# Fused causal attention and SwiGLU FFN on one core: normalised x transposed by DMA instead of on TensorE, with its stages spread over the FFN groups

## The chip, the cores and the metric

The kernel runs on one core of a Trainium2 chip. The metric is the device time of one execution in microseconds (us). Most executions of one kernel agree within a fraction of a per cent; medians are quoted.

Engines are named as in the profile: PE is TensorE (matmul), PEld its weight loads, DVE is VectorE, ACT is ScalarE, POOL is GpSimd, SP is SyncE, which here only issues DMAs. "L359" is a line of the kernel that the view belongs to; the same statement has another number in another version. A lower-case q (SPq, POOLq) is the sequencer or DMA queue of that engine. A DMA lands when its data have arrived. "Half clock" is a stretch in which the granted PE clock is 0.5.

## The reference

Eight batches of causal attention, eight heads each, 576 positions, head dimension 64. A decay bias is added to the scores. The outputs of all heads of a position form one row of 512 numbers; the 4608 rows go through an RMS norm and a SwiGLU FFN (512 to 1536 to 512).

```python
def _attn_ref(q, k, v, s):
    scores = scale * np.matmul(q, k.transpose(0, 1, 3, 2))
    s_pos = np.maximum(s, 0.0)
    cum = np.cumsum(s_pos, axis=-1)
    bias = -(cum[:, :, :, None] - cum[:, :, None, :])
    scores = np.where(causal, -1000000000.0, scores + np.minimum(bias, 0.0))
    ...                                     # softmax over keys, then attn @ v

def _moe_ref(x, w_gate, w_val, w_out, rms_g):
    rms = np.sqrt(np.mean(x * x, axis=-1, keepdims=True) + 1e-06)
    xn = x / rms * rms_g
    g = xn @ w_gate
    silu = g * (1.0 / (1.0 + np.exp(-g)))
    val = xn @ w_val
    return (silu * val @ w_out).astype(np.float32)
```

## The kernel before

The kernel is a chain of nine stages. Stage c (0 to 8) is one FFN chunk of 512 rows. It has two parts. In the first, FFN1, PE computes gate and value products in 12 groups of 16 matmuls (a group covers 256 hidden units for 256 rows in the "halves" plan, so groups 0 to 5 need the chunk's first 256 rows and groups 6 to 11 the last 256; in the "whole" plan a group covers all 512 rows). In the second, 48 output matmuls are interleaved with the attention of batch c+1: scores, exp, mask, attention times V. A batch has 576 rows and a chunk 512, so chunk c can start when the first rows of batch c are normalised; the rest are normalised while FFN1 already runs.

The way of a block of 128 rows from attention to FFN1: x_blk holds the attention output with rows on the partitions. ACT squares and sums it, POOL takes the power -1/2, DVE scales it, and then it must be turned so that the model dimension lies on the partitions (xnT), because FFN1 contracts over that dimension. Before the change PE turns it, by four transposing matmuls into PSUM, and DVE copies it out with rms_g multiplied in:

```python
def att_square(a, tb):
    nc.scalar.activation(out=sq_scr[:, 0:DM], in_=a.x[:, tb, :], func=AF.Square,
                         accum_out=a.ss[:, tb : tb + 1])

def att_alpha(a, t0, t1):
    ...                                              # POOL: mean + eps, then
    nc.gpsimd.tensor_tensor(out=y, in0=m, in1=mhalf[:, 0 : t1 - t0], op=ALU.pow)

def att_scale(a, tb):
    nc.vector.tensor_scalar(out=a.x[:, tb, :], in0=a.x[:, tb, :],
                            scalar1=a.al[:, 1, tb : tb + 1], scalar2=None, op0=ALU.mult)

def att_out(a, tb):
    p0 = 64 if tb == 4 else 0
    X = ps_x()                                       # PSUM
    for cc in range(CC):
        nc.tensor.matmul(X[:, cc, :], lhsT=a.x[:, tb, cc * 128 : (cc + 1) * 128],
                         rhs=ident_bf, is_transpose=True,
                         start=(cc == 0), stop=(cc == CC - 1))
    c0 = a.b * S + tb * 128
    nc.vector.tensor_tensor(
        out=xnT[:, :, c0 : c0 + 128 - p0], in0=X[:, :, p0:128],
        in1=g_sb.unsqueeze(2).to_broadcast([128, CC, 128 - p0]), op=ALU.mult)

def ffn1_group(Ht, t0, o, n, f0):
    ...
    nc.tensor.matmul(P[:, j, i * n : (i + 1) * n],
                     lhsT=w[:, cc, fb * 128 : (fb + 1) * 128],
                     rhs=xnT[:, cc, t0 + o : t0 + o + n], ...)
```

Everything that is not PE work of the FFN is a "filler": a pair of a position (0 to 1 through FFN1) and a function, emitted after the FFN1 group at that position. In a stage c, POOL issues the loads of k and q of batch c+2, SP the loads of v, POOL scales v of batch c+1 by the decay (`prep_v`), and SP issues two large DMA transposes that turn K and Q of batch c+1 (`dma_transpose`):

```python
elif c + 1 < B:
    fillers += prep_fillers(c + 1, 0.4, 0.98)       # prep_v on POOL at 0.2 to 0.8
    ...
    for w in range(2):
        dma_transpose(c + 1, w)                      # K and Q, at the stage's start
if c + 2 < B:
    for w in range(2):
        fillers.append((0.1, lambda b=c + 2, w=w: load_kq(b, w)))   # five issues each, POOL
    fillers.append((0.1, lambda b=c + 2: load_v(b, nc.sync)))       # five issues, SP
...
Ht = ffn1(c, halves if c < 4 else whole, fillers)
```

## Time and profile before

| | before |
|---|---|
| time, median of three runs | 396.05 us (395.88 to 397.04) |
| span of the profiled run | 394.0 us |
| PE busy | 355.1 us, 90% |
| mean granted PE clock | 0.989 |
| first FFN1 matmul (end of the load phase) | 29.0 us |
| stage 0 / stages 1 to 5 / stage 6 | 55.2 / 39.5 to 39.7 each / 41.4 us |

The page's first part gives busy time and share of the span for each engine. Its second part cuts the span into 40 slices; a digit is the busy share in tenths, and in the row PEclk it is the clock granted to PE, in tenths of full speed.

```profile
PE 355.1 (90%) x2870; PEld 210.5 (53%) x2907; DVE 219.9 (56%) x438; ACT 203.6 (52%) x327; POOL 172.0 (44%) x267
...
PE   2779993999999999999999999999979999999993
...
PEclk9999999799999999999999999999999999999998
```

PE is the bottleneck: from the fourth slice on it is over 90% busy everywhere, except in the last slice, in the 30th (a wait of 2.0 us for H_sb in stage 6) and in the seventh, which is very poor. The waits view of PE, where a line says how long PE sat idle in front of an instruction and which instruction ended it, says what that slice is:

```profile
PE psAV L322 <- POOL E L300: 7.2, 2, 7.0
...
PE psX L351 <- DVE x_blk L327: 4.6, 7, 0.7
PE psD L366 <- DVE H_sb L373: 2.0, 1, 2.0
```

One wait of 7.0 us lies in stage 0, where POOL masks E only after it has scaled v, and v had landed late. The granted clock falls after it (the 7 in the PEclk row). Otherwise a stage's waits are short: the transposes into psX wait some 0.66 us for the last attention output.

The timeline of PE in stage 3 shows what the transposes cost. The columns are start, duration, engine, line, operation, output and inputs, count.

```profile
167.01 0.39 PE L351 MATMUL psX<-ident_bf,x_blk 128*128 128x128 bf16 x4
167.42 1.03 PE L366 MATMUL psD<-xnT,wg_sb 128*128 128x256 bf16 x8
...
169.17 0.39 PE L351 MATMUL psX<-ident_bf,x_blk 128*128 128x128 bf16 x4
169.39 1.04 PE L366 MATMUL psD<-xnT,wg_sb 128*128 128x256 bf16 x8
...
201.69 0.40 PE L351 MATMUL psX<-ident_bf,x_blk 128*128 128x128 bf16 x4 [0.66 <-DVE x_blk L327]
```

Eight matmuls of 256 columns take 0.87 us from start to start; four transposes push the next group back by 0.22 us (169.17 to 169.39), or 0.41 in the first of these lines (167.01 to 167.42). There are five blocks in a batch and eight batches. A saving of 9 us of issue, with the gaps round the last two blocks of each stage, is what the change can hope for on PE.

### The profile page before, as it was taken

The page shows a single profiled execution, that of the slowest core. Times are in us where ns is not written, and L with a number is a line of the kernel's source. Part 1 is how long each engine was busy: PE and PEld are TensorE (multiplying, and loading weights), DVE is VectorE, ACT ScalarE, POOL GpSimd, SP SyncE. Part 2 cuts the span into 40 slices and gives each one's busy share as a digit, 9 for nine tenths or more (in the row PEclk, how much of TensorE's full clock was granted, in tenths as well). Part 3 has the DMA queues.
Part 4 walks back from the last instruction along what each step waited for, and adds up shares of the span by engine and source line. Part 5 has one row for each costly group of instructions (what it writes and reads, how often), then busy time and mean ns, then how long its engine had stood idle before and what let it go on. Part 6 is the DMA issues. An engine that isn't in the chain of part 4 may idle for free.

```text
span 394.0 us, 7348 instructions
## 1 busy us (share of the span) xinstructions
PE 355.1 (90%) x2870; PEld 210.5 (53%) x2907; DVE 219.9 (56%) x438; ACT 203.6 (52%) x327; POOL 172.0 (44%) x267
## 2 busy tenths in 40 slices
PE   2779993999999999999999999999979999999993
PEld 1457871469746974698454445444434454444441
DVE  6774960675377546754675467546763585424431
ACT  2664564564486448644864486458635773302310
POOL 8553639459145924592459245924540240000000
PEclk9999999799999999999999999999999999999998
DMA  8999999039923992299529932993260010011011
GB/s 118 212 202 169 196 209 141 28 88 154 176 66 85 147 175 79 66 152 142 126 72 155 171 85 72 152 171 89 69 119 2 27 56 29 0 56 52 0 45 71
DMA packets 128905, 41.60 MB, mean 106 GB/s; under 512 B 116960, under 2 KB 123616, under 8 KB 128864
## 3 DMA queue, kind: packets, MB, share of 16 engines
q0 software_dynamic: 63840, 16.52, 48.1%
q1 hardware_dynamic: 65024, 24.53, 31.5%
q8 instruction: 25, 0.41, 0.4%
q14 instruction: 16, 0.13, 0.1%
HBM read 37.90 MB, written 9.44 MB: 120 GB/s over the span
## 4 chain that ended last, share of the span: by engine, by line
PE 71%; POOL 8%; DMA 7%; ACT 6%; DVE 5%; issue 2%; POOLq 0%; ACTq 0%
PE psD L366 41%; PE psO L394 18%; DMA v_nat<-in_v_dram 7%; PE psAV L322 6%; PE psD L293 4%; ACT E L298 2%; ACT L298 2%; ACT sq_scr L334 2%; DVE x_blk L344 2%; PE psX L351 2%; POOL v_nat L118 1%; POOL E L300 1%; POOL vw L258 1%; DVE x_blk L327 1%; POOL xnT L111 1%
## 5 line engine op out<-in xcount | busy, mean ns | idle before, releaser
L373 DVE TENSOR_TENSOR H_sb<-S_sb,psD 128x512 bf16<-128x512 bf16 x108 | 74.1, 687 | 93.6 <-ACT S_sb L372 93.3
L372 ACT ACTIVATE S_sb<-psD 128x512 bf16<-128x512 f32 x108 | 64.4, 597 | 114.8 <-PE psD L366 105.5
L366 PE MATMUL psD<-xnT,wg_sb 128*128 128x256 bf16 (+1 forms) x615 | 111.5, 315 | 2.9 <-DVE H_sb L373 2.0
L366 PE MATMUL psD<-xnT,wv_sb 128*128 128x256 bf16 (+1 forms) x623 | 112.0, 315 | 0.3
L394 PE MATMUL psO<-wout_sb,H_sb 128*128 128x512 bf16 x405 | 103.0, 382 | 1.4
L300 POOL TENSOR_SCALAR_AFFINE_SELECT E<-E 128x512 bf16<-128x512 bf16 x64 | 40.6, 636 | 98.0 <-ACT E L298 95.2
L366 PEld LDWEIGHTS <-wv_sb 128*128 128x128 bf16 x624 | 61.4, 98 | 33.1
L366 PEld LDWEIGHTS <-wg_sb 128*128 128x128 bf16 x624 | 60.4, 99 | 34.0 <-issue 2.5
L298 ACT ACTIVATE E<-psD 128x1024 bf16<-128x1024 f32 x64 | 63.7, 1023 | 17.8 <-PE psD L293 17.5
L394 PEld LDWEIGHTS <-H_sb 128*128 128x128 bf16 x432 | 37.7, 98 | 36.9 <-issue 3.5
L399 DVE COPY osb<-psO 128x512 f32<-128x512 f32 x36 | 24.8, 688 | 30.3 <-PE psO L394 28.6
L322 PE MATMUL psAV<-vw,E 128*128 128x65 bf16 x576 | 32.9, 202 | 9.7 <-POOL E L300 7.2
L322 PEld LDWEIGHTS <-E 128*128 128x128 bf16 x576 | 24.4, 102 | 21.6 <-POOL E L300 14.0
L258 POOL TENSOR_TENSOR vw<-v_nat,wT 128x512 bf16<-128x512 f32 (+1 forms) x35 | 35.4, 1047 | 0.1
L334 ACT ACTIVATE sq_scr<-x_blk 128x512 bf16<-128x512 bf16 x40 | 25.1, 628 | 18.1 <-DVE x_blk L327 17.3
L327 DVE TENSOR_TENSOR x_blk<-psAV,rZ 128x256 bf16<-128x256 f32 (+1 forms) x64 | 31.4, 491 | 2.2
L105 POOL DMA_DIRECT2D k_nat<-in_k_dram x30 | 25.8, 873 | 9.2 <-DMA wout_sb<-in_moe_w_out_dram 6.4
L293 PE MATMUL psD<-QT,KT 64*128 64x256 bf16 (+2 forms) x384 | 27.2, 252 | 1.3 <-ACT E L298 0.9
L293 PEld LDWEIGHTS <-KT 64*128 64x128 bf16 x384 | 13.2, 99 | 27.2 <-issue 25.8
L326 DVE RECIPROCAL rZ<-psAV 128x4 f32<-128x4 f32 (+1 forms) x64 | 11.8, 184 | 28.0 <-PE psAV L322 27.7
L105 POOL DMA_DIRECT2D q_nat<-in_q_dram x30 | 25.4, 870 | 3.6 <-DMA k_nat<-in_k_dram 1.7
L244 DVE TENSOR_REDUCE peak<-QT 128x1 f32<-128x640 bf16 (+1 forms) x32 | 25.3, 792 | 0.0
(77 smaller groups left out, 218.5 us busy)
## 6 DMA issues: line engine op xcount, KB each, us to landing
out_dram<-osb SPq DMA_DIRECT2D x36, 256.0 KB, 2.0
v_nat<-in_v_dram SPq DMA_DIRECT2D x24, 256.0 KB, 10.1
k_nat<-in_k_dram POOLq DMA_DIRECT2D x24, 128.0 KB, 7.6
q_nat<-in_q_dram POOLq DMA_DIRECT2D x24, 128.0 KB, 12.6
v_nat<-in_v_dram POOLq DMA_DIRECT2D x8, 256.0 KB, 12.2
wg_sb<-in_moe_w_gate_dram POOLq DMA_DIRECT2D x2, 768.0 KB, 15.1
wv_sb<-in_moe_w_val_dram POOLq DMA_DIRECT2D x2, 768.0 KB, 18.9
wout_sb<-in_moe_w_out_dram POOLq DMA_DIRECT2D x2, 768.0 KB, 13.1
```

Source lines behind the costliest of these rows:

```text
L105: nc.gpsimd.dma_start(out=dst[0:n, b % 2, sc, :, :], in_=src[b, :, sc * 128 : sc * 128 + n, :].rearrange("h p d -> p h d"))
L258: eng.tensor_tensor(out=vw[0:n, sc, :, 0:64], in0=v_nat[0:n, b % 2, sc, :, :], in1=wb.unsqueeze(2).to_broadcast([n, H, D]), op=ALU.mult)
L293: nc.tensor.matmul(st[:, j, c0 : c0 + q1 - q0], lhsT=keys(a.b, rs, hp, kb), rhs=queries(a.b, rs, hp, q0, q1), start=(i == 0), stop=(i == l ...
L298: nc.scalar.activation(out=E, in_=st, func=AF.Exp, scale=0.125)
L300: nc.gpsimd.affine_select(out=diag, in_=diag, pattern=[[0, 4], [1, 128]], compare_op=ALU.is_ge, fill=0.0, base=0, channel_multiplier=-1)
L322: nc.tensor.matmul(AV[:, j, qb - q0, :], lhsT=E[:, j, c0 : c0 + 128], rhs=vw[:, kb, h, :], start=(j == 0 and i == 0), stop=(j == 1 and i = ...
L327: nc.vector.tensor_tensor(out=a.x[:, q0 : q0 + nq, hp * 128 : (hp + 1) * 128].rearrange("p t (j d) -> p j t d", j=2), in0=AV[:, :, :, 0:64 ...
L334: nc.scalar.activation(out=sq_scr[:, 0:DM], in_=a.x[:, tb, :], func=AF.Square, accum_out=a.ss[:, tb : tb + 1])
L366: nc.tensor.matmul(P[:, j, i * n : (i + 1) * n], lhsT=w[:, cc, fb * 128 : (fb + 1) * 128], rhs=xnT[:, cc, t0 + o : t0 + o + n], start=(i = ...
L372: nc.scalar.activation(out=sl, in_=P[:, 0, :], func=AF.Silu)
L373: nc.vector.tensor_tensor(out=Ht[:, f0 : f0 + m, o : o + n], in0=sl.rearrange("p (i n) -> p i n", i=m), in1=P[:, 1, :].rearrange("p (i n) ...
L394: nc.tensor.matmul(O, lhsT=Ht[:, fb, tb * 128 : (tb + 1) * 128], rhs=wout_sb[:, fb, :], start=(fb == 0), stop=(fb == FB - 1))
```

## The change

The intent is to take the 160 transposes off PE and their evictions off DVE. SP issues a DMA transpose from SBUF to SBUF for each block; rms_g is then applied in the scaling on DVE, as a row broadcast to all partitions. A DMA transpose takes longer to come back, so squares, power and scaling are spread over the early FFN1 groups ("stages"), and loads are moved. The first loads of stage 0 move from position 0.1 to 0.25. The rest of the diff, cut to what matters:

```diff
     def att_scale(a, tb):
-        nc.vector.tensor_scalar(out=a.x[:, tb, :], in0=a.x[:, tb, :],
-                                scalar1=a.al[:, 1, tb : tb + 1], scalar2=None, op0=ALU.mult)
+        nc.vector.scalar_tensor_tensor(out=a.x[:, tb, :], in0=a.x[:, tb, :],
+                                       scalar=a.al[:, 1, tb : tb + 1], in1=g_row,
+                                       op0=ALU.mult, op1=ALU.mult)

     def att_out(a, tb):
         p0 = 64 if tb == 4 else 0
-        X = ps_x()
-        ... four transposing matmuls, eviction on DVE with g_sb ...
+        nc.sync.dma_start_transpose(out=xnT[:, :, c0 : c0 + 128 - p0], in_=a.x[p0:128, tb, :])

+    def table(func):
+        nc.scalar.activation(out=dummy[:, 1:2], in_=dummy[:, 0:1], func=func)
+
+    def attention(b, fl):
+        early = {1: 2, 2: 1, 3: 1}.get(b, 0)
+        a = att_begin(b)
+        table(AF.Exp)                     # the table load, early
+        ... scores now in pairs, AV in pairs, output matmuls between ...
+            if early and u == HP:
+                for tb in range(early):
+                    att_square(a, tb)
+                att_alpha(a, 0, early)
+                for tb in range(early):
+                    att_scale(a, tb)
+                    att_out(a, tb)
+        table(AF.Silu)
+        take(fl, 48)
+        return a
+
+    stages = {0: ((2, 3, 4), ()), 1: ((2, 3, 4), ()), 2: ((1, 2), (3, 4)), 3: ((1, 2), (3, 4))}
+    def tail_fillers(a):                  # default of stages: ((0, 1), (2, 3, 4))
+        f = []
+        g = 0
+        for st in stages.get(a.b, ((0, 1), (2, 3, 4))):
+            if not st:
+                continue
+            for i, tb in enumerate(st):
+                f.append((g + i, lambda tb=tb: att_square(a, tb)))
+            g += len(st) - 1
+            f.append((g, lambda st=st: att_alpha(a, st[0], st[-1] + 1)))
+            for i, tb in enumerate(st):
+                f.append((g + 1, lambda tb=tb: [att_scale(a, tb), att_out(a, tb)]))
+            g += 2
+        return [((p + 0.9) / 12, fn) for p, fn in f]
...
+                if c == 1:
+                    fillers.append((0.3, lambda: load_v(2, nc.sync)))
                 for w in range(2):
-                    dma_transpose(c + 1, w)
+                    fillers.append((0.4, lambda b=c + 1, w=w: dma_transpose(b, w)))
             if c + 2 < B:
                 for w in range(2):
-                    fillers.append((0.1, lambda b=c + 2, w=w: load_kq(b, w)))
-                fillers.append((0.1, lambda b=c + 2: load_v(b, nc.sync)))
+                    fillers.append(((0.24, 0.6)[w], lambda b=c + 2, w=w: load_kq(b, w)))
+                if c:
+                    fillers.append((0.85, lambda b=c + 2: load_v(b, nc.sync)))
...
-            Ht = ffn1(c, halves if c < 4 else whole, fillers)
+            Ht = ffn1(c, halves if c < B else whole, fillers)
```

v of batch 1 is now scaled on DVE, that of later batches on POOL at positions 0.62 to 0.9; `E` gets eight buffers instead of seven.

More of the change, by code (lines that the diff above doesn't have):

```diff
@@ L60 @@
     g_sb = pers.tile([128, CC], fp32, name="g_sb")
+    g_row = pers.tile([128, DM], fp32, name="g_row")
     s_all = pers.tile([BH, S], fp32, name="s_all")
@@ L78 @@
     knrm = pers.tile([128, 1], fp32, name="knrm")
-    mhalf = pers.tile([128, 3], fp32, name="mhalf")
+    mhalf = pers.tile([128, NB], fp32, name="mhalf")
     hones = pers.tile([128, 2], fp32, name="hones")
@@ L83 @@
     ok1 = pers.tile([BH, 2], fp32, name="ok1")
+    dummy = pers.tile([1, 2], fp32, name="dummy")
     flag = pers.tile([1, 1], i32, name="flag")
@@ L93, in ps_av @@
         return pp.tile([128, 2, nq, 65], fp32, name="psAV", tag="AT", bufs=2)
-    def ps_x():
-        return pp.tile([128, CC, 128], bf16, name="psX", tag="AT", bufs=2)
     def ps_t():
@@ L296, in unit_scores @@
                     start=(i == 0), stop=(i == len(groups) - 1))
-        E = a.E[u] = mp.tile([128, 2, DM], bf16, name="E", tag="E", bufs=7)
+        E = a.E[u] = mp.tile([128, 2, DM], bf16, name="E", tag="E", bufs=8)
         nc.scalar.activation(out=E, in_=st, func=AF.Exp, scale=0.125)
@@ L343, in att_scale @@
     def att_scale(a, tb):
-        nc.vector.tensor_scalar(out=a.x[:, tb, :], in0=a.x[:, tb, :],
-                                scalar1=a.al[:, 1, tb : tb + 1], scalar2=None, op0=ALU.mult)
+        nc.vector.scalar_tensor_tensor(out=a.x[:, tb, :], in0=a.x[:, tb, :],
+                                       scalar=a.al[:, 1, tb : tb + 1], in1=g_row,
+                                       op0=ALU.mult, op1=ALU.mult)
     def att_out(a, tb):
         p0 = 64 if tb == 4 else 0
-        X = ps_x()
-        for cc in range(CC):
-            nc.tensor.matmul(X[:, cc, :], lhsT=a.x[:, tb, cc * 128 : (cc + 1) * 128],
-                             rhs=ident_bf, is_transpose=True,
-                             start=(cc == 0), stop=(cc == CC - 1))
         c0 = a.b * S + tb * 128
-        nc.vector.tensor_tensor(
-            out=xnT[:, :, c0 : c0 + 128 - p0], in0=X[:, :, p0:128],
-            in1=g_sb.unsqueeze(2).to_broadcast([128, CC, 128 - p0]), op=ALU.mult)
+        nc.sync.dma_start_transpose(out=xnT[:, :, c0 : c0 + 128 - p0], in_=a.x[p0:128, tb, :])
     def ffn1_group(Ht, t0, o, n, f0):
@@ L415, in prep_fillers @@
         f += spread([lambda i=i: prep_norm(b, i) for i in range(3)], lo, hi)
-        f += spread([lambda sc=sc: prep_v(b, sc, nc.gpsimd) for sc in range(NB)], 0.2, 0.8)
-        f.append((0.8, lambda: prep_w(b, nc.gpsimd)))
-        return f
-    def tail_fillers(a, steps):
-        return [(p, lambda tb=tb: att_out(a, tb)) for p, tb in zip(steps, (2, 3, 4))]
+        f += spread([lambda sc=sc: prep_v(b, sc, nc.vector if b < 2 else nc.gpsimd) for sc in range(NB)],
+                    *((0.62, 0.9) if b > 1 else (0.99, 1.0)))
+        f.append((0.95, lambda: prep_w(b, nc.gpsimd if b > 1 else nc.scalar)))
+        return f
     def take(filler, n):
@@ L425, in take, with attention_first @@
             next(filler, None)
-    def attention(b, filler, lead, each):
-        a = att_begin(b)
-        take(filler, lead[0])
+    def attention_first():
+        a = att_begin(0)
         unit_scores(a, 0)
-        take(filler, lead[1])
         unit_scores(a, 1)
-        take(filler, lead[2])
         for u in range(2 * HP):
@@ L444, in attention @@
                     att_scale(a, tb)
-                if not each:
-                    for tb in (0, 1):
-                        att_out(a, tb)
-            if b and u < HP:
-                prep_peak(b, u)
-            take(filler, each[u] if each else 0)
-        if each:
-            for tb in (2, 3, 4):
-                att_square(a, tb)
-            att_alpha(a, 2, 5)
-        if each:
-            for tb in (0, 1):
-                att_out(a, tb)
-            for _ in filler:
-                pass
-            for tb in (2, 3, 4):
-                att_scale(a, tb)
@@ L462, in attention @@
-        return a
+                for tb in (0, 1):
+                    att_out(a, tb)
[6 more added lines that the diff above has]
+        table(AF.Exp)
+        take(fl, 8)
+        unit_scores(a, 0)
+        unit_scores(a, 1)
+        take(fl, 10)
+        for u in range(0, 2 * HP, 2):
+            if u + 2 < 2 * HP:
+                unit_scores(a, u + 2)
+                unit_scores(a, u + 3)
+            else:
+                take(fl, 5)
+            unit_av(a, u)
+            if u < HP:
+                prep_peak(b, u)
+            take(fl, 2)
+            unit_av(a, u + 1)
+            if u < HP:
+                prep_peak(b, u + 1)
+            if early and u == HP:
[4 more added lines that the diff above has]
+                    att_scale(a, tb)
+                    att_out(a, tb)
+            take(fl, 3)
+        table(AF.Silu)
+        take(fl, 48)
+        return a
@@ L470 @@
         nc.sync.dma_start(out=g_sb, in_=moe_rms_g.rearrange("(cc p) -> p cc", p=128))
+        nc.sync.dma_start(out=g_row, in_=moe_rms_g.unsqueeze(0).to_broadcast([128, DM]))
         load_runs(0, 0, 0, 4)
@@ L481 @@
         nc.vector.memset(ones, 1.0)
+        nc.vector.memset(dummy, 0.0)
         nc.vector.memset(w_row[:, S : NB * 128], 0.0)
@@ L503 @@
             prep_v(0, sc, nc.vector)
-        a = attention(0, iter(()), (0, 0, 0), None)
+        a = attention_first()
         for c in range(NCH):
@@ L507 @@
             if c < B:
-                fillers += tail_fillers(a, (0.33, 0.41, 0.49) if c == 0 else (0.16, 0.25, 0.33))
+                fillers += tail_fillers(a)
             if c == 0:
-                fillers += [(0.0, lambda: [att_square(a, tb) for tb in (2, 3)]),
-                            (0.09, lambda: (att_square(a, 4), att_alpha(a, 2, 5))),
-                            (0.24, lambda: [att_scale(a, tb) for tb in (2, 3, 4)])]
                 fillers += spread([lambda hp=hp: prep_peak(0, hp) for hp in range(HP)], 0.3, 0.6)
@@ L521 @@
                           lambda: load_v(1, nc.gpsimd)):
-                    fillers.append((0.1, f))
+                    fillers.append((0.25, f))
             elif c + 1 < B:
+                if c == 1:
+                    fillers.append((0.3, lambda: load_v(2, nc.sync)))
                 for w in range(2):
-                    dma_transpose(c + 1, w)
+                    fillers.append((0.4, lambda b=c + 1, w=w: dma_transpose(b, w)))
             if c + 2 < B:
                 for w in range(2):
-                    fillers.append((0.1, lambda b=c + 2, w=w: load_kq(b, w)))
-                fillers.append((0.1, lambda b=c + 2: load_v(b, nc.sync)))
+                    fillers.append(((0.24, 0.6)[w], lambda b=c + 2, w=w: load_kq(b, w)))
+                if c:
+                    fillers.append((0.85, lambda b=c + 2: load_v(b, nc.sync)))
             if c == B:
                 fillers += spread([check_decay] + check_all(), 0.0, 0.9)
-            Ht = ffn1(c, halves if c < 4 else whole, fillers)
+            Ht = ffn1(c, halves if c < B else whole, fillers)
             fl = ffn2_steps(c, Ht)
             if c + 1 < B:
-                a = attention(c + 1, fl, (8, 4, 6), (3, 3, 3, 3, 3, 3, 6, 0))
+                a = attention(c + 1, fl)
             else:
```

## The prediction

> **What bounds it now.** TensorE (PE). The busy table gives PE 355 of 394 us; DVE, ACT and POOL are at 44 to 56%. In the PE timeline the kernel is a load stage (to 29 us), a disturbed first FFN-plus-attention stage (29.0 to 84.1, 55 us), six steady stages of 39.5 to 41.5 us, then two FFN stages (31.7, 32.5). A steady stage: 192 gate/value matmuls of 512 columns at 0.216 us, or their halves (20.8), 48 output matmuls (10.4), scores (2.6), attention-value (2.2), five transposes of x, 0.22 us of issue per block of four (1.1). That sums to 37; the other 2.5 are gaps: about 1.4 us round the two block transposes at the end of attention (0.66 us waits for x_blk among them), the rest at switches between scores, AV and FFN.
>
> In the disturbed stage the waits view shows one PE wait of 7.0 us (AV for affine_select): POOL scales v behind queued k/q load issues, v having landed near 60. The windows table then grants clocks 0.76 and 0.56 from 65 to 75 us, some 4 us more.
>
> **Removed.** 160 PE transposes (40 blocks x 0.22 = 9 us of PE issue) with their gaps (6 x about 1.4), and 24.5 us of DVE evictions, off the path. Table loads (1.28 us, as the Trainium skill, "ScalarE: Activation LUTs", What ACT_TABLE_LOAD costs, states too) are 2% of the chain of waits, but PE runs output matmuls meanwhile: under 2 us. Scaling v(1) on DVE, v(2) loaded later, fewer POOL issues in front: most of the 7 + 4 us.
>
> **Added.** 40 DMA transposes of 128x512 on the SP queue. The 640 KB K transposes take 3.3 us to issue and 5.2 to 10.1 to land. I estimate 0.7 us issue and 2.5 to 3.5 to landing for 128 KB, 4 to 6 beside loads, since all queues share 16 engines ("DMA: Bandwidth & Descriptors", Issuing engines are not separate DMA queues). DVE scaling with g: 0.37 to about 0.6 us, free.
>
> Deadlines: blocks staged after FFN group 2 or 3 must land by group 6, 10.4 us after the stage's start; squares, pow, scaling and landing end near 10.5 to 12.5. "Early" blocks have some 4.6 us of PE work behind them and need 7 to 9. In stage 1 the v(2) load sits ahead of the transposes on SP (five issues, 11 us now), so group 6 and the K/Q transposes come late. In stage 0 the first FFN group waits for two transposes amid weight loads (2 to 4 us), group 6 for two more.
>
> **Sum of savings.** Stage 0: +11 gain less 7 new waits = 4. Stage 1: -2. Stages 2, 3: 1.5 each. Stages 4, 5: 2.7 each. Stage 6: 4 (its 2.0 us DVE wait goes too). Tail: 0.4. About 15 us: **381 us**, 8 in 10 between **369 and 392**. Chances: faster 0.79, same 0.16, slower 0.05.
>
> **What would show it.** Right: no 7 us AV wait; stages 4 to 6 near 37 us; PE waits for DMA of xnT confined to stages 0 to 3, some 10 us in total; x transposes landing in 2.5 to 6 us; table loads away from the chain at no gain for PE. Wrong: steady stages still 39, or xnT waits in stages 4 to 6.
>
> **What would make it wrong.** Transposes landing quickly even under load (then 370); or transposes blocking on SP behind loads and output stores, so that every stage waits at group 6; or PE gaps that lower the granted clock, as after the 7 us wait; or paired scores making PE wait for exp (two exps, 2.05 us, against 2.1 us of PE work).

## The result, and the profile after

The change made the kernel slower. The median of four runs is 441.72 us (441.48 to 442.88) against 396.52 us (395.88 to 397.04) for the kernel before on the same chip. Ratios in this document are the mean time of one kernel's runs over that of the other's of the same rounds, so they are not quite the ratio of the quoted medians. Here it is 1.1147, with a 95% interval of 1.1118 to 1.1175. Executions over 1.5% slower than the fastest of the same kernel are left out of the means.

Cutting both PE timelines at the first gate matmul of each stage gives this table (us; the last stage ends with the span):

```text
           start   c0    c1    c2    c3    c4    c5    c6    c7    c8   span
before      29.0  55.2  39.7  39.7  39.7  39.5  39.5  41.4  31.8  38.6  394.0
after       36.4  62.5  48.9  44.7  43.5  46.0  47.6  41.3  32.0  37.9  440.9
difference  +7.4  +7.3  +9.2  +5.0  +3.8  +6.5  +8.1  -0.1  +0.2  -0.7  +46.9
```

The loss is not in one place. Every stage up to 5 loses 4 to 9 us, stage 0 and its start 15 us, and stage 6 nothing. Stage 6 does the same FFN work as stages 4 and 5, and it will be the key.

The page after, in the same parts as shown of before:

```profile
PE 358.0 (81%) x3100; PEld 249.5 (57%) x3131; DVE 218.7 (50%) x404; ACT 202.6 (46%) x343; POOL 174.0 (39%) x264
...
PE   1756548949499959996999589967999799999994
...
PEclk9999859988889988998899889998899899999998
```

PE's busy time is nearly the same (358.0 against 355.1 us) although 160 transposes are gone, and the row PEclk, which was nearly all 9, has an 8, and once a 5, in 12 of the first 26 slices. Both say that a part of the matmuls ran slowly. The waits view of PE says where the idle time is:

```profile
PE psD L359 <- DMA xnT<-x_blk: 45.8, 9, 11.3
PE psD L359 <- DVE H_sb L366: 7.6, 5, 3.0
...
PE psD L359 <- issue: 4.4, 1, 4.4
```

The 7.0 us wait for POOL is gone, as intended. In its place PE waits nine times, 45.8 us in all, for a DMA transpose of x. (The line "issue" is a tenth wait of the same kind: it lies at group 6 of stage 5, and the transposes of x landed at its end.)

### One stage, read line by line

Stage 4 starts at 236.04. These are lines of the timeline of the changed kernel; a bracket gives the idle time in front of the instruction and what ended it, and the SPq lines are the time in which SP issued, not the transfer.

```profile
236.04 1.04 PE L359 MATMUL psD<-xnT,wg_sb 128*128 128x256 bf16 x8
...
241.30 0.71 POOL L340 TENSOR_TENSOR al<-al,mhalf 128x2 f32<-128x2 f32 x1
...
241.98 4.32 POOL L104 DMA_DIRECT2D k_nat<-in_k_dram  x5
...
242.71 1.41 DVE L343 SCALAR_TENSOR_TENSOR x_blk<-x_blk,al,g_row 128x512 bf16<-128x512 bf16 x2
...
243.48 3.47 SPq L350 DMA_TRANSPOSE xnT<-x_blk  x2
...
245.64 1.04 PE L359 MATMUL psD<-xnT,wv_sb 128*128 128x256 bf16 x8
...
247.19 4.63 SPq L238 DMA_TRANSPOSE KT<-k_nat  x1
...
251.90 1.86 PE L359 MATMUL psD<-xnT,wg_sb 128*128 128x256 bf16 x8 [5.22 <-DMA xnT<-x_blk]
...
253.56 1.91 PE L359 MATMUL psD<-xnT,wv_sb 128*128 128x256 bf16 x8
253.92 5.98 POOL L257 TENSOR_TENSOR vw<-v_nat,wT 128x512 bf16<-128x512 f32 x5
...
255.27 1.80 PE L359 MATMUL psD<-xnT,wg_sb 128*128 128x256 bf16 x8
...
256.74 3.71 DVE L343 SCALAR_TENSOR_TENSOR x_blk<-x_blk,al,g_row 128x512 bf16<-128x512 bf16 x3
256.90 1.04 PE L359 MATMUL psD<-xnT,wv_sb 128*128 128x256 bf16 x8
...
261.10 1.03 PE L359 MATMUL psD<-xnT,wg_sb 128*128 128x256 bf16 x8 [1.41 <-DVE H_sb L366]
```

Five things are to be read here.

1. The power of the first two blocks is done at 242.0, and the next thing that POOL does is to issue the five loads of k. The x transposes are issued by SP from 243.48 on, so the loads start ahead of them and run beside them.
2. PE has finished group 5 at about 246.7 and resumes at 251.90, 15.9 us after the stage's start. The prediction put this at 10.5 to 12.5.
3. When PE resumes, a block of eight matmuls takes 1.66, 1.71 and 1.63 us from start to start instead of 0.87. The differences add up to 2.4 us, and the granted clock between 251.9 and 258.6 was 0.63. The Trainium skill, "TensorE: Matmul & The Clock Gate", Part 1: The HAM clock gate, states that after an idle window of about 3.4 us PE runs at half clock until it has been busy for as long. This trace agrees for the wait of 5.22 us; the slow matmuls behind it lasted 5.0 us (251.90 to 256.90).
4. The three scalings of the second part of x take 3.71 us on DVE while POOL scales v, instead of the 0.7 us apiece of the first two. They sit in front of the H_sb products that FFN1 needs, and PE waits 1.41 us for these.
5. The K transpose behind the x transposes is issued from 247.19 for 4.63 us, so its issue ends at 251.82, just as PE resumes. That coincidence held within 0.3 us in all of stages 1 to 5 and gave the rival theory below.

The sum for stage 4: 5.2 of wait, 2.4 of half clock, and 1.6 round the H_sb wait, less 0.6 for the transposes that are gone from FFN1 (21.6 before, 21.0 for the unstalled groups now) and less 2.4 in the attention part (17.9 before, 15.5 now), make 6.2; the stage lost 6.5. The gain that was hoped for is there, and it is given back three times over.

The view of one line's instructions in a window gives the landing times. First the x transposes of stage 4, then those of stage 6, in the changed kernel:

```profile
L350 SPq DMA_TRANSPOSE xnT<-x_blk x2: 1238/1690/2143, 243.5 to 244.8; - x2
...
DMA to landing us min/median/max: 6.2/6.6/7.0
...
L350 SPq DMA_TRANSPOSE xnT<-x_blk x2: 1208/1225/1242, 337.1 to 338.4; - x2
...
DMA to landing us min/median/max: 2.4/2.4/2.5
```

The first line of each pair has the issue time on SP in ns (least, median, most), the second the time from issue to landing. The same two transposes, issued the same 7.4 us after the stage's start, land after 6.2 to 7.0 us in stage 4 and after 2.4 in stage 6. Stage 6 has no loads of k and q, because batch 8 doesn't exist; it does have the K and Q transposes behind. It has no wait for x at all. In stage 0, where x runs beside the loads of weights, k, q and v, landing took 8.5 to 11.0 us, and the wait at group 6 was 11.27 us.

### The profile page after: what moved, and what is told of

The parts are those of the page before. It is cut to its first block, busy times and chain, and to the rows that moved or that the text cites. A ratio compares the mean times of both kernels' runs of the same rounds, so it can differ in the third digit from the quotient of the medians.

```text
span 440.9 us, 7872 instructions
## 1 busy us (share of the span) xinstructions
PE 358.0 (81%) x3100; PEld 249.5 (57%) x3131; DVE 218.7 (50%) x404; ACT 202.6 (46%) x343; POOL 174.0 (39%) x264
## 4 chain that ended last, share of the span: by engine, by line
PE 58%; DVE 15%; DMA 15%; issue 4%; ACT 3%; POOL 2%; SPq 0%; POOLq 0%; ACTq 0%
PE psD L359 38%; PE psO L387 15%; DMA xnT<-x_blk 13%; DVE x_blk L343 6%; DVE peak L243 3%; PE psD L292 2%; PE psAV L321 2%; DMA xnT<-in_q_dram 2%; DVE x_blk L326 2%; ACT S_sb L365 1%; DVE H_sb L366 1%; DVE osb L392 1%; ACT E L297 1%; DVE vw L257 1%; POOL E L299 1%
## 5 line engine op out<-in xcount | busy, mean ns | idle before, releaser
L359 PE MATMUL psD<-xnT,wg_sb 128*128 128x256 bf16 (+1 forms) x814 | 125.5, 301 | 57.9 <-DMA xnT<-x_blk 45.8
L359 PEld LDWEIGHTS <-wg_sb 128*128 128x128 bf16 x816 | 84.9, 105 | 82.5 <-issue 54.5
L359 PE MATMUL psD<-xnT,wv_sb 128*128 128x256 bf16 (+1 forms) x816 | 121.0, 294 | 0.0
L387 PE MATMUL psO<-wout_sb,H_sb 128*128 128x512 bf16 x403 | 99.9, 379 | 1.2
L359 PEld LDWEIGHTS <-wv_sb 128*128 128x128 bf16 x816 | 84.5, 104 | 19.2
L338 POOL TENSOR_SCALAR al<-ss 128x2 f32<-128x2 f32 (+2 forms) x18 | 3.5, 196 | 95.7 <-ACT sq_scr L333 95.5
L343 DVE SCALAR_TENSOR_TENSOR x_blk<-x_blk,al,g_row 128x512 bf16<-128x512 bf16 x40 | 37.2, 974 | 2.3 <-POOL al L340 2.3
L257 POOL TENSOR_TENSOR vw<-v_nat,wT 128x512 bf16<-128x512 f32 (+1 forms) x30 | 33.5, 1177 | 0.0
L321 PE MATMUL psAV<-vw,E 128*128 128x65 bf16 x576 | 30.4, 200 | 3.3 <-DVE x_blk L326 1.6
L292 PE MATMUL psD<-QT,KT 64*128 64x256 bf16 (+2 forms) x384 | 22.7, 248 | 1.8 <-ACT E L297 0.9
## 6 DMA issues: line engine op xcount, KB each, us to landing
v_nat<-in_v_dram POOLq DMA_DIRECT2D x8, 256.0 KB, 12.4
wg_sb<-in_moe_w_gate_dram POOLq DMA_DIRECT2D x2, 768.0 KB, 12.4
```

Of the source, the lines that this page charges most:

```text
L257: eng.tensor_tensor(out=vw[0:n, sc, :, 0:64], in0=v_nat[0:n, b % 2, sc, :, :], in1=wb.unsqueeze(2).to_broadcast([n, H, D]), op=ALU.mult)
L321: nc.tensor.matmul(AV[:, j, qb - q0, :], lhsT=E[:, j, c0 : c0 + 128], rhs=vw[:, kb, h, :], start=(j == 0 and i == 0), stop=(j == 1 and i = ...
L343: nc.vector.scalar_tensor_tensor(out=a.x[:, tb, :], in0=a.x[:, tb, :], scalar=a.al[:, 1, tb : tb + 1], in1=g_row, op0=ALU.mult, op1=ALU.mult)
L359: nc.tensor.matmul(P[:, j, i * n : (i + 1) * n], lhsT=w[:, cc, fb * 128 : (fb + 1) * 128], rhs=xnT[:, cc, t0 + o : t0 + o + n], start=(i = ...
L387: nc.tensor.matmul(O, lhsT=Ht[:, fb, tb * 128 : (tb + 1) * 128], rhs=wout_sb[:, fb, :], start=(fb == 0), stop=(fb == FB - 1))
```

## The experiments

**Theory.** The DMA transposes of x land late because POOL's loads of k and q start just before them. The Trainium skill, "DMA: Bandwidth & Descriptors", Issuing engines are not separate DMA queues, states that DMAs of all issuing engines run on the same 16 DMA engines and interleave. Each late landing costs PE its wait and then the half clock.

**Rivals.** (a) The K transpose, issued on the same queue right behind, holds the x transposes up. (b) The DMA transposes are not to blame; it is the rest of the change, the new staging of squares and scalings. (c) The waits are small change, and the half clock is the loss.

### e1: the change with TensorE transposes

Everything of the change stays, but blocks are turned by PE again, two groups after their scaling (the early ones at the end of the attention), with a plain copy out of PSUM.

```diff
-        nc.sync.dma_start_transpose(out=xnT[:, :, c0 : c0 + 128 - p0], in_=a.x[p0:128, tb, :])
+        X = ps_x()
+        ... four transposing matmuls ...
+        nc.vector.tensor_copy(out=xnT[:, :, c0 : c0 + 128 - p0], in_=X[:, :, p0:128])
```

> The changed kernel with only the 40 DMA transposes undone: TensorE transposes x again (already scaled by g) and VectorE copies it out; everything else of the change stays. Theory (the loss is the wait for the DMA transposes plus the slow clock after it): no PE wait over 2 us at the middle of a stage, granted clock back near 0.98, time 372 to 385 us. Rival (the paired scores, the 256-column halves in all stages or the moved loads cost the time): still above 400 us.

Measured: 395.57 us, ratio 0.9979 (0.9935 to 1.0023), so the same as before. The expectation of 372 to 385 was missed. Against the change it is 46 us less: the DMA transposes are what makes the changed kernel slow, and rival (b) falls. Yet the rest of the change gained nothing in this form, since new waits took its gain. The waits view of e1:

```profile
PE psX L354 <- DVE xnT L358: 12.9, 6, 3.0
```

Transposes placed three in a row after one group need a PSUM buffer that DVE hasn't emptied.

### e2: k and q loads later

```diff
-                    fillers.append((0.3, lambda: load_v(2, nc.sync)))
+                    fillers.append((0.45, lambda: load_v(2, nc.sync)))
...
-                    fillers.append(((0.24, 0.6)[w], ...load_kq...))
+                    fillers.append((((0.5, 0.75) if c else (0.24, 0.6))[w], ...load_kq...))
```

> The changed kernel with the k and q loads of the batch after next (and the early v load of stage 1) issued only after the x transposes, in the second half of a stage. Theory (the x transposes are slow because they share the DMA engines with these loads): in stages 2 to 5 their landing falls from 5.3 to 7.0 us towards 2.4, the wait at group 6 from 4.4 to 5.2 us to about 1 us, total 415 to 425 us. Rival 1 (landing is held up by the K/Q transposes that follow on the same queue): waits unchanged. Rival 2 (the chain squares, pow, scale, issue is too long even without contention): waits fall by less than half.

Measured: 410.7 us (the median with the slow execution; 409.89 without it), ratio 1.0374 (1.0318 to 1.043), a little better than expected. No instruction was taken away; only the loads moved, those of k by three FFN1 groups or about 5 us, and 31 us came back. Between the two profiles 25.6 us of the gain lie in stages 2 to 5. Another 4.0 us lie in stage 0, which the edit doesn't touch, and say nothing of the loads: with the same code, stage 0 took 58.5 to 62.5 us in the profiles of the change, e2, e3, e5 and e6. The x transposes that e2 issues in stage 2 for its group 6, in the same view as above:

```profile
DMA to landing us min/median/max: 2.4/2.4/2.5
```

In stages 2 to 6 the blocks needed at group 6 land in 2.4 to 3.2 us. In stages 2 and 3 the stage is 38.4 and 37.5 us instead of 44.7 and 43.5. This is the theory's main test and it held. Two things stayed. Stage 0 was not touched. Stage 1 (47.8) was, but POOL had nothing else to do there and issued the k loads at 103.88, right after the power and 1.4 us ahead of the first x transpose, which then took 5.3 us to land: a later position in the program is no later issue on an engine that runs ahead.

### e3: K and Q transposes later

```diff
-                    fillers.append((0.4, lambda b=c + 1, w=w: dma_transpose(b, w)))
+                    fillers.append((0.58, lambda b=c + 1, w=w: dma_transpose(b, w)))
```

> The changed kernel with the K and Q transposes of the next batch issued after group 6 in place of group 4, loads where they were. PE resumed each time within 0.2 us of the end of the K transpose's issue, so the rival says that the K transpose behind them holds the x transposes up: then the wait at group 6 falls to about 1 us. Theory (the loads do it, and the K issue is merely held up by the same loads): wait at group 6 still 4 to 5 us; the total is the same or a little longer, as K and Q come later for the scores.

Measured: 441.94 us, ratio 1.1168 (1.1126 to 1.1211), the changed kernel again. SP's timeline of stage 4, and the PE line behind the wait:

```profile
241.36 18.15 SPq L350 DMA_TRANSPOSE xnT<-x_blk  x5
259.74 2.51 SPq L238 DMA_TRANSPOSE KT<-k_nat  x1
...
249.26 1.87 PE L359 MATMUL psD<-xnT,wg_sb 128*128 128x256 bf16 x8 [4.70 <-DMA xnT<-x_blk]
```

All five x transposes of the stage are now ahead of the K transpose, which comes 10 us after PE resumed, and the wait at group 6 is still 4.70 us. Rival (a) falls: the coincidence of times is not the cause of the wait.

### e4: no wait for x at all (a wrong result)

FFN1 reads the gate weights in place of xnT. The transposes all run as in the change, but no matmul waits for them.

```diff
-                                     rhs=xnT[:, cc, t0 + o : t0 + o + n],
+                                     rhs=wg_sb[:, cc, o : o + n],
```

> Wrong result on purpose: gate and value matmuls read loaded weights in place of xnT, so that PE never waits for x; all squares, scales, DMA transposes and loads still run. Theory: everything lost is the wait and the clock after it, so 368 to 382 us, granted clock near 0.98. Rival: if the other parts of the change are slow by themselves, it stays above 396 us.

Measured: 392.42 us, ratio 0.9898 (0.9846 to 0.995). Waiting for x, with what follows from it, costs 49 us of the changed kernel, more than its whole loss. But 368 to 382 was missed. The waits view of e4:

```profile
PE psD L292 <- DMA QT<-q_nat: 11.6, 5, 3.1
...
PE psD L359 <- DVE H_sb L366: 6.0, 11, 2.5
```

With FFN1 shorter, PE comes to the scores before the Q transpose has landed, and waits there. That is why this run cannot be read as what the change would be worth with fast transposes: a wait taken away shows the next one. The wait for the Q transpose is new, and its 11.6 us are more than the 10.4 by which the run missed the expected range; the waits for H_sb were there before (7.6 us).

### e5: PE kept busy during the wait

25 matmuls of 384 columns on loaded weights, into a PSUM buffer that nobody reads, in front of group 6 of stages 1 to 5.

```diff
         for i, (o, n, f0) in enumerate(plan):
+            if i == 6 and 1 <= c <= 5:
+                W = pp.tile([128, 384], fp32, name="psWarm", tag="AT", bufs=2)
+                for r in range(25):
+                    nc.tensor.matmul(W, lhsT=wg_sb[:, 0, 0:128], rhs=wg_sb[:, 1, 0:384],
+                                     start=True, stop=True)
             ffn1_group(Ht, c * DM, o, n, f0)
```

> The changed kernel with 25 needless 384-column matmuls (about 4 us) in front of group 6 of stages 1 to 5, where PE otherwise waits 4.4 to 6.5 us for x. They lengthen nothing if they fit in the wait. Theory (a wait of over 4 us makes the next 4 us of matmuls run at half speed, 1.7 us for 8 instead of 0.87): group 6 starts at the same time but runs at full speed, about 2.2 us saved in each of the five stages, 430 to 434 us. Rival (the slow matmuls come from something else than the idle time): no gain or longer.

Measured: 436.02 us, ratio 1.1019 (1.0981 to 1.1057); 430 to 434 was expected. Stage 4 in the timeline of e5:

```profile
236.94 4.23 PE L378 MATMUL psWarm<-wg_sb 128*128 128x384 bf16 x25
241.78 1.03 PE L359 MATMUL psD<-xnT,wg_sb 128*128 128x256 bf16 x8 [0.61 <-DMA xnT<-x_blk]
...
251.51 1.87 PE L359 MATMUL psD<-xnT,wg_sb 128*128 128x256 bf16 x8 [4.33 <-DVE H_sb L366]
```

Group 6 ran at full speed (1.03 instead of 1.86 for the eight matmuls), and stages 1 to 3 became shorter by 2.3 to 2.7 us each: the half clock after a wait is a cost of its own, some 2 us a time. In stage 4 PE then ran into the H_sb wait, 4.33 us long, and fell to half clock after all; all H_sb waits of the run make 12.4 us (7.6 in the change), and the expected range was missed by 2 us. Rival (c) falls as the main cause: keeping the clock up brought (1.1147 - 1.1019) times 396, some 5 us of the 45, in this run.

### e6: e2, with v scaled at the start of a stage

The H_sb waits stood beside POOL's scaling of v, so v of batches 3 and later is scaled at position 0.0 instead of 0.62 to 0.9. Nothing else differs from e2.

```diff
+        lo_v, hi_v, at_w = ((0.99, 1.0, 0.95), (0.62, 0.9, 0.95), (0.0, 0.01, 0.02))[
+            0 if b < 2 else 1 if b < 3 else 2]
```

> As e2_loads_later, and POOL scales v for the next batch at the start of stages 2 to 6 in place of their second half. Scaling x on VectorE took 0.75 us beside nothing and 1.1 to 2.3 us beside that POOL work, and PE then waited up to 3 us for H_sb. Theory (POOL and VectorE slow each other, which hurts where x is scaled late): the waits for H_sb in stages 4 to 6 vanish, 2 to 3 us less in each, 402 to 406 us. Rival: the waits stay, since x is scaled before H_sb on VectorE anyway.

Measured: 407.71 us, ratio 1.0298 (1.0262 to 1.0334), 3 us less than e2 and 1.7 above the expected range of 402 to 406. The waits view of e6, for H_sb, where e2 had 7.4 us:

```profile
PE psD L359 <- DVE H_sb L366: 1.8, 5, 0.5
```

Stages 4, 5 and 6 became shorter by 2.7, 0.8 and 2.3 us. (That the run gained less fits the start and stages 0 and 1, which have the same code as in e2 and came out 3.1 us longer in this profile.) The 40 scalings of x of each kernel, sorted by what POOL did meanwhile, give the reason (only the two clearest cases are shown, 3 and 3 scalings before, 9 and 9 after):

```text
scaling of x on DVE, mean ns (least to most)   POOL idle         POOL scales v
before (tensor_scalar, one tensor input)       351 (348-354)     1123 (1122-1125)
after  (two tensor inputs, x and g)            747 (743-752)     1534 (815-2339)
```

Stages 2 to 6 of e6 are 39.2, 37.5, 38.7, 38.1 and 37.3 us. That comes close to what the prediction had said for stages 4 to 6, "near 37", once the loads are kept out of the way at the right moment.

### b1: e6, with batches 0 and 1 turned by PE

For stages 0 and 1 the x transposes of the change took 4.6 to 11.0 us to land, so the blocks of these two batches are turned by PE, one a group; v of batch 2 is loaded in stage 0 again and scaled at the start of stage 1, and the load of the rms_g row is moved out of the way of the first loads.

```diff
+        if a.b > 1:
+            nc.sync.dma_start_transpose(out=xnT[:, :, c0 : c0 + 128 - p0], in_=a.x[p0:128, tb, :])
+            return
+        X = ps_x()
+        ... as in e1 ...
```

> An attempt to beat both: as e6, but batches 0 and 1, whose blocks fall into the heavy loads, go through TensorE transposes, spread one per group; v for batch 2 is loaded in stage 0 as before; the load of g comes behind the first loads. Stages 2 to 6 should take 37 to 38 us, stage 0 about 47, stage 1 about 40: 371 to 380 us.

Measured: 385.33 us, ratio 0.973 (0.9703 to 0.9757), faster than both kernels, but 5 us above the expected range (stage 0 took 52.0 us where about 47 was expected, stage 1 43.8 where about 40 was). From e6 it is 22.4 us: the start and stage 0 give 17 of them, stage 1 gives 4.6. In front of stage 1, 2 us before it starts, PE waits 2.5 us for the early blocks, and the granted clock is then 0.50 from 78.8 to 85.6, mostly inside stage 1 (it starts at 80.1). The waits view of b1 says:

```profile
PE psX L361 <- DVE x_blk L329: 2.8, 2, 2.5
```

The squares of the early blocks end late in the attention of batch 1, their scalings then stand on DVE in front of the last attention outputs (L329), and the transposes wait for these. b3 takes that up.

### b2: b1, with all batches turned by PE

```diff
     def on_pe(b):
-        return b < 2
+        return True
```

> As b1_mixed, but all blocks go through TensorE. It tells what the DMA transposes are worth where nothing contends with them: five transposes of 0.22 us of issue and their copies, so 1 to 1.5 us a stage in six stages, 377 to 386 us, some 7 us over b1_mixed. If it is as fast as b1_mixed, the DMA transposes buy nothing even there.

Measured: 396.66 us, ratio 1.0017 (0.9991 to 1.0043). With all else equal, the DMA transposes of batches 2 to 7 are worth (1.0017 - 0.973) times 396, that is 11 us. The expectation was missed here too: "take the change's other parts and keep PE's transposes" is no better than before. This holds for my placement of the transposes (14.1 us of waits for xnT from DVE); a better one was not searched for.

### e7: the change, with batches 0 and 1 alone turned by PE

```diff
-        nc.sync.dma_start_transpose(...)
+        if a.b > 1:
+            nc.sync.dma_start_transpose(...)
+            return
+        X = ps_x()
+        ... as in e1 ...
```

> The changed kernel with batches 0 and 1 alone on TensorE transposes (one per group, after their scaling); loads and all else as the change has them, DMA transposes from batch 2 on. Theory: the first part of the loss (first FFN group 7.5 us late, stages 0 and 1 together 16.5 us longer than before the change) comes from DMA transposes amid weight, v and k/q loads, so about 25 us come back: 412 to 420 us, stages 2 to 6 as slow as in the change (43 to 48 us). Rival: stages 0 and 1 are slow for other reasons (v loaded later, scores paired), then less than 10 us come back.

Measured, with the PE transposes one a group: 416.47 us, ratio 1.0538 (1.0491 to 1.0585), as expected. The load stage ends at 30.4, stages 0 and 1 take 50.8 and 42.3 us; stages 2 to 5 keep the 43 to 48 us of the change. Stage 2 starts at 123.4 us, where it started at 123.8 in the kernel before and at 147.8 with the change. So 24 of the 45 us are lost before stage 2, by the DMA transposes of batches 0 and 1, and stages 2 to 5 account for the rest. That it is the loads which delay the transposes there too fits the landing times of 8.5 to 11.0 us, but no run moved the loads of stage 0.

### e8: the kernel before, with DMA transposes alone

```diff
 # kernel before; scaling with g_row, and
     def att_out(a, tb):
-        ... four transposing matmuls, eviction ...
+        nc.sync.dma_start_transpose(out=xnT[:, :, c0 : c0 + 128 - p0], in_=a.x[p0:128, tb, :])
```

> The kernel before with one part of the change alone: x scaled with g on VectorE and 40 DMA transposes at the places of the TensorE ones, no staging. Blocks then come due for the first FFN group right after they are issued, and stand behind the K/Q transposes on the SP queue. Theory: worse than the whole change, 440 to 470 us, PE waits for xnT in every stage. If it is below 430 us, the staging of the change cost more than it saved.

Measured: 462.69 us, ratio 1.1718 (1.1677 to 1.176), as expected. The change's other parts are thus worth (1.1718 - 1.1147) times 396, some 23 us, where DMA transposes are used; they were needed, and not enough. SP's timeline of stage 2 of e8, which starts at 148.5:

```profile
160.31 12.03 SPq L119 DMA_DIRECT2D v_nat<-in_v_dram  x5
172.44 2.62 SPq L352 DMA_TRANSPOSE xnT<-x_blk  x2
```

Here the x transposes stand behind five loads of v on the same queue, whose issue alone takes 12 us. This is a second way to be late, and the changed kernel avoids it in most stages by loading v at 0.85.

### e9: b1 without the early table loads

```diff
-        table(AF.Exp)
...
-        table(AF.Silu)
```

> b1_mixed without the table loads issued early. The prediction put their worth under 2 us: 385 to 388 us (b1_mixed 385.3). If what the chain of waits shows of them (7 loads of 1.28 us) were all lost time, it would be 9 us longer, 394 us.

Measured: 390.96 us, ratio 0.9888 (0.9856 to 0.9921), over the expected range. Loading the tables early is worth (0.9888 - 0.973) times 396, some 6 us, not under 2. The waits view of e9:

```profile
PE psD L295 <- ACT E L300: 4.6, 8, 0.9
```

This line was 0.9 us in b1, and the waits for H_sb were 1.9 us there against 3.8 here. A likely reason, not tested further, is that scores now come in pairs and their exps close behind one another, so that a table load of 1283 ns in front of the first one is not hidden any more.

### b3: b1, with the early squares before the last scores

```diff
+            if early and u == HP:             # before unit_scores(6), (7)
+                for tb in range(early):
+                    att_square(a, tb)
+                att_alpha(a, 0, early)
             if u + 2 < 2 * HP:
                 unit_scores(a, u + 2)
                 unit_scores(a, u + 3)
...
             if early and u == HP:
                 for tb in range(early):
-                    att_square(a, tb)
-                att_alpha(a, 0, early)
-                for tb in range(early):
                     att_scale(a, tb)
```

> b1_mixed with the squares of the early blocks of batches 1 to 3 ahead of the last two exps on ScalarE, not behind them. PE waits 3.4 us in all at the end of stage 0 and 1.4 to 1.5 us at the starts of stages 2 and 3; these should go, with the half-speed matmuls after the first: 378 to 383 us.

Measured: 379.95 us, ratio 0.9604 (0.9582 to 0.9626), as expected, and the fastest of all: 4% under the kernel before and, by the ratios, 5 us under b1. In the profiles stage 1 fell from 43.8 to 40.5 us, while stage 0 grew from 52.0 to 53.6, with a clock of 0.50 from 76.6 to 80.0 there instead; the line for psX shown of b1 is gone. (The profiled execution, 382.6 us, is the longest of the six of b3, so its stages show less of the gain than the ratio.) Its page:

```profile
PE 347.1 (91%) x3171; PEld 243.6 (64%) x3171; DVE 214.2 (56%) x414; ACT 202.6 (53%) x343; POOL 171.4 (45%) x265
...
PEclk9988999989999999999999999999999999999999
```

Its waits view has 2.5 us left of the 45.8 us for x:

```profile
PE psD L373 <- DMA xnT<-x_blk: 2.5, 4, 0.7
```

And its stage 4 can be laid beside that of the change. It starts at 197.81:

```profile
205.25 2.53 SPq L357 DMA_TRANSPOSE xnT<-x_blk  x2
...
209.15 1.03 PE L373 MATMUL psD<-xnT,wg_sb 128*128 128x256 bf16 x8 [0.70 <-DMA xnT<-x_blk]
...
211.41 4.30 POOL L107 DMA_DIRECT2D k_nat<-in_k_dram  x5
```

The x transposes are issued 7.44 us after the stage's start, to a hundredth as in the change. PE resumes at 11.3 us instead of 15.9, at full clock. What differs for these transposes is that the loads of k are issued from 211.41, after they have landed. The blocks of the second part, issued beside the loads, still take 6.4 to 8.6 us to land in stages 2 to 5, and nobody waits for them.

The stages of the kernels that matter most, in us:

```text
           start   c0    c1    c2    c3    c4    c5    c6    c7    c8
before      29.0  55.2  39.7  39.7  39.7  39.5  39.5  41.4  31.8  38.6
after       36.4  62.5  48.9  44.7  43.5  46.0  47.6  41.3  32.0  37.9
e2          36.0  58.5  47.8  38.4  37.5  41.5  38.9  39.6  32.0  37.9
e6          37.0  60.0  48.4  39.2  37.5  38.7  38.1  37.3  32.0  38.0
b1          28.0  52.0  43.8  39.1  37.4  38.2  38.1  37.3  32.0  37.6
b3          28.1  53.6  40.5  38.3  37.4  38.2  38.1  37.3  32.0  37.5
```

## Why the prediction was wrong

It said 381 us with a range of 369 to 392, and gave "slower" a chance of 0.05. The time was 441.72. Its sum, taken apart by stage, against the spans:

```text
                     predicted   measured   missed by
start and stage 0        -4        +14.8       18.8
stage 1                  +2         +9.2        7.2
stages 2 and 3           -3         +8.8       11.8
stages 4 and 5           -5.4      +14.6       20.0
stage 6                  -4         -0.1        3.9
stages 7 and 8           -0.4       -0.4        0
sum                     -14.8      +46.9       61.7
```

**The step that failed first is the landing time under load.** The prediction put "2.5 to 3.5 to landing for 128 KB, 4 to 6 beside loads", and it knew of the shared engines. Alone it is 2.4 us, so the first half was right. Beside the loads of k and q it was 5.3 to 7.0 us in stages 2 to 5, and beside the loads of stage 0 up to 11.0. The issue on SP was 1.2 us for each block where 0.7 was estimated. The worse slip is the term built from it: for "squares, pow, scaling and landing end near 10.5 to 12.5" the prediction seems to have used the quiet landing, although the diff puts the loads of k at position 0.24, just there: the second x transpose was issued 8.8 us after the start of stage 4, and its own estimates make that 11.3 to 12.3 us with the quiet landing and 12.8 to 14.8 beside loads. With quiet engines the term is right (11.3 us in b3); in the changed kernel PE resumed 15.0 to 15.9 us after the start of stages 2 to 5. So stages 2 to 5 waited 4.4 to 5.2 us each where 0 to 2 had been expected, and nothing at all was expected of stages 4 and 5. e2 shows this by moving the loads alone.

**Stage 0's new waits were foreseen, but they were far too small in the sum, so that a gain of 4 became a loss of 14.8.** "Less 7 new waits" was measured as 7.1 and 11.3 us, 18.4 in all. The gain of 11 that was set against it was hoped to come from the 7.0 us wait and its slow clock. That wait did go, but a gain of 11 was not seen in any run: where PE turns the blocks of stage 0 (e1, b1, b2, e7), the start and stage 0 are 3.0 to 4.3 us shorter than before, with other waits in them.

**The half clock after each wait was left out of the sum.** It was named among the things that would make the prediction wrong ("PE gaps that lower the granted clock") but had no number. It costs about 2.4 us after each wait for x, as the line-by-line reading showed and e5 confirmed for stages 1 to 3. Stage 6 shows it even behind a wait of 2.51 us for H_sb: the blocks of eight matmuls after it took 1.13, 1.71 and 1.45 us from start to start.

**"0.37 to about 0.6 us, free" was wrong about the scaling on DVE.** It took 0.75 us alone and 1.5 in the mean beside POOL's scaling of v, in front of the H_sb products. Moving that work of POOL away brought 2.7, 0.8 and 2.3 us in stages 4 to 6 (e2 against e6). The slowed scaling is also why the 2.0 us H_sb wait of stage 6 did not go, as had been predicted, but became a longer one; in e6 no H_sb wait is longer than 0.5 us. The trace fits two statements of the Trainium skill. "VectorE: DVE Perf Modes", Mode 2×_2P, says that an operation with a single tensor input can use both read ports and run at twice the rate, and that one with two tensors can't (0.35 to 0.75 us here). "SBUF — State Buffer", SBUF: two separate sides, says that such a DVE operation and a GpSimd operation that reads SBUF exclude one another for the whole instruction. The table under e6 agrees with it (the scaling grew by 0.77 us before and 0.79 after, where one POOL scaling of v takes about 1 us); no run here isolated the ports as such.

**"Under 2 us" for the early table loads was too small.** b1 against e9 gives 6 us. The load itself takes 1283 ns in the trace, as the page that the prediction names has it; what it costs probably depends on what stands behind it, which no run tested.

**What was right.** The 7.0 us wait went. The attention part became 1.3 to 1.4 us shorter in stages 1 and 2 and 2.2 to 2.4 in stages 3 to 6. The tail gained 0.4. Stages 2 to 6 come to 37 to 39 us where nothing is in the way (e6, b3), so the gain of some 2 us a stage that the prediction counted on was real, and the DMA transposes of batches 2 to 7 are worth 11 us against TensorE transposes placed as in b2. The change failed by where its transfers were put, not by what it removed from PE.

**What stays open.** Whether TensorE transposes, placed better than in e1 and b2, could come as far as b3. Whether the loads are what delays the x transposes of stage 0. And how e4's time divides, since new waits took the place of the old ones.

## What to carry to other kernels

A transfer that replaces work on the busiest engine is a latency with a deadline, and its latency has to be read for the moment at which it will run: look in the trace for what else will be in flight then, and read a transfer of that size from a stage that has it in flight too, not the quiet one. When a wait of some microseconds is added to TensorE, add the slow clock behind it as well (2.4 us here after 5 us). And when a change looks bad, try moving the neighbours of the new transfer before undoing it: five microseconds of delay to loads that had time to spare brought back 31 of 45 us, 25.6 of them in stages 2 to 5.

## What the Trainium skill lacked or had wrong

- "DMA: Bandwidth & Descriptors" has no latency for a small DMA transpose from SBUF to SBUF on this chip, and the time for one of 128 by 128 in "VectorE: DVE Perf Modes", The three transpose paths, does not say what else was in flight. Here one of 128 by 512 bf16 elements (128 KB) took 1.2 us to issue on SP and 2.4 us to landing with quiet engines, 5.3 to 7.0 beside loads of k and q, and up to 11.0 beside loads of weights. One of 640 KB took 2.5 us to issue quietly and 4.6 to 5.7 beside loads.
- The same page, in Issuing engines are not separate DMA queues, calls the time to initiate a DMA usually small against the DMA. For these transposes it was half of the quiet landing time (1.2 of 2.4 us), and five v loads held SP for 12.03 us in e8.
- "TensorE: Matmul & The Clock Gate", Part 1, gives an idle window of about 3.4 us for the fall to half clock. In the changed kernel it fell behind a wait of 2.51 us too (granted clock 0.63 between 348.4 and 353.0); behind the wait of 2.0 us in stage 6 of the kernel before it did not (1.00 from 282.5 to 322.0). The wait of 5.22 us agrees with the page.
- "SBUF — State Buffer", Who interferes with whom, mentions slowdowns of 6.8 times for DVE and 1.5 times for GpSimd, without the operations that they were measured on. Here a DVE scaling of 0.75 us took 1.5 us in the mean, and up to 2.3, beside POOL's scaling of v.
